# Tile 0's attention reordered on hand-assigned PSUM banks, and tile 1's query and key loaded once

## The chip, the cores and the metric

The kernel runs on one core of one Trainium2 chip. A core has five engines that work side by side and meet only at semaphores: TensorE (PE, matrix multiplies into PSUM), VectorE (DVE), ScalarE (ACT), GpSimd (POOL) and SyncE (SP). The metric is the device time of one execution in microseconds; lower is better. PSUM, where matmuls put their results, has eight banks of 128 partitions by 512 fp32 numbers in this kernel's use of it.

## What is computed

Sliding-window causal attention over 8 batches, 8 heads, 576 positions and head size 64 (window 64), followed by a gated feed-forward block on its 4608 x 512 result.

```python
scores = scale * np.matmul(q, k.transpose(0, 1, 3, 2))
rel = pos[:, None] - pos[None, :]
mask = (rel >= 0) & (rel < window)
scores = np.where(mask, scores, -1000000000.0)
attn = np.exp(scores - max); attn = attn / sum(attn)
x = np.matmul(attn, v)            # heads side by side: 4608 x 512
g = x @ w_gate
return (g / (1 + np.exp(-g)) * (x @ w_val)) @ w_out    # 512 -> 1536 -> 512
```

(`max` and `sum` stand for the row maximum and row sum.) Inputs and output are fp32; the kernel multiplies in bf16 and accumulates in fp32.

## The kernel before

The 4608 tokens are nine tiles of 512. Tiles 0 to 6 and 8 are the first 512 positions of a batch, tile 7 collects the last 64 positions of all eight. For each tile there is an attention stage (scores, exponential, totals, values) and a feed-forward stage: twelve gate groups m, each four matmuls for `g_ps` and four for `v_ps` (L412), then the projection `o_ps` (L421) with twelve steps c. Attention of tile t+1 is threaded between the projection matmuls of tile t.

The kernel runs under a manual schedule: every engine executes its instructions in the order in which the program text issues them. So a line's place in the text is its place in the engine's queue, and an instruction that waits holds up all behind it on that engine.

*Heads go in four pairs u = 0 to 3.* Tile 0 is special. Its q and k arrive as fp32 (`raw`), are cast to bf16 by ACT, DVE or POOL (`cast_first`), turned by PE against an identity matrix (`turn_pe`, L186) and copied out of PSUM into `qT` and `kT` (L546, L189). `scores_first` puts a bias matmul (L221, -1e9 outside the window) and 16 score matmuls (L230) into a two-bank tile and lets ACT exponentiate it. `log_of` and the lines before it form the totals with a matmul of ones (L287); ACT takes logarithm and then exp(-x), so that a multiplication replaces the division. `values_first` multiplies with the values (L337) and DVE scales the result into `xT` (L370). The value matmuls of tile 0 use blocks of 128 keys that begin either at a multiple of 128 (`v1`) or 64 rows before one (`v2`). `v2` is a copy of `v1` shifted by 64 partitions, made by `shift_pair` (L167, L168).

*Matmuls of ones* (`keep_warm`, L493) whose results nobody reads stand at some places of the opening.

*Tile 1.* Its key comes as `raw_k`, 128 partitions by heads, in bf16 by a converting DMA. During gate groups m = 5 to 9 of tile 0, ACT rearranges it (`join` into `keys`), PE turns it (L186, four transposes between two gate groups) and DVE copies it into `kT[1]`. Its query comes as `q_s` and is turned by DVE's 32 x 32 stream transpose (L198, `turn_q`) at m = 9, 10, 11 and after m = 11. That transpose needs the second 32 columns of each head on partitions 32 to 63 (and 96 to 127) at columns 0 to 31. So `load_q` sends the query twice: in four quarters, where the quarters c = 1 read the same rows from column 32 on. From tile 2 on the key is loaded in the same manner (`load_k`) and turned by DVE (L208, `turn_k`).

After the twelve groups of tile 0 comes the passage into tile 1, on PE in this order: `scores(1, 0)` (pairs 0 and 1), `columns(0, 4)` (16 projection matmuls), `scores(1, 1)` (pairs 2 and 3), `columns(4, 7)`, totals, `columns(7, 10)`, values, `columns(10, 12)`. For each `scores` call ACT exponentiates two tiles and DVE multiplies with the mask (L277) and adds (L282).

*PSUM* is given out by two pools: `ps_a` with two buffers of two banks (`wide`), `ps_f` with two tags "g" and "v" of two single banks each. A request takes the buffer of its tag that was asked for longest ago and waits until its readers are done.

*Loads.* POOL issues the weight and tile loads in the order of the text (L172, L74, L88, L178, L137); SP issues tile 0's q, k and half of v. Eight loads of POOL can be under way; the ninth waits for the first.

Of the kernel before, what the change touches and what calls it, by code (L numbers as in the profile page):

```python
# [8 lines left out]
P = 128  # L9
# [8 lines left out]
def kernel(  # L18
# [24 lines left out]
    hpool = ctx.enter_context(tc.tile_pool(name="hpool", bufs=2))  # L43
    ps_a = ctx.enter_context(tc.tile_pool(name="ps_a", bufs=2, space=PSUM))
    ps_f = ctx.enter_context(tc.tile_pool(name="ps_f", bufs=2, space=PSUM))

# [4 lines left out]
    v12 = cst.tile([P, 2, 4, H, D], BF16, name="v12")  # L51
    v1, v2 = v12[:, 0], v12[:, 1]
    vl = v12[:].rearrange("r g i (c w h) d -> r (g i) c w h d", c=2, w=2)
# [4 lines left out]
    tri = cst.tile([P, 2, 64], BF16, name="tri")  # L58
    bias = cst.tile([P, 2, 4, 4, 2, 16], BF16, name="bias")
    mask = cst.tile([P, 8, 2, 16, 4], BF16, name="mask")  # L60

# [19 lines left out]
    def load_q(t):  # L81

        q_s = stage.tile([P, 4, 16 * D], BF16, name="q_s", tag="q")
        w = 16 * D - 32
# [15 lines left out]
        return q_s  # L100

    def load_k(k_s, groups):

# [11 lines left out]
    def load_qk(t):  # L115
        q_s = load_q(t)
        if t == 1:
            staged[t] = q_s, None
            return
        if t == LAST:  # L120
# [42 lines left out]

    def shift_pair(u):
        hs = slice(2 * u, 2 * u + 2)
        a, b = v1[:, :, hs], v2[:, :, hs]
        nc.vector.tensor_copy(b[64:128, 1:4], a[64:128, 0:3])  # L167
        nc.vector.tensor_copy(b[0:64], a[0:64])  # L168

    def weights_gv(f0, f1, c0=0, c1=4):  # L170
# [41 lines left out]

    def scores_first(u):

        qT = queries[0][:, u, :]
        E = eb[u][:, 1:17].rearrange("r (h y) z -> r h (y z)", h=2)
        s_ps = wide("s_ps")
        for c in range(2):
            for h in range(2):
                r = slice(64 * h, 64 * h + 64)  # L220
                nc.tensor.matmul(  # L221
                    s_ps[64 * c:64 * c + 64, h], identb[r, r],
                    bias[r, c ^ h].rearrange("r e i c x -> r (e i c x)"),
                    start=True, stop=False,
                )
        for j in range(8):
            c = j % 2
            for h in range(2):
                r = slice(64 * h, 64 * h + 64)
                nc.tensor.matmul(  # L230
                    blocks(s_ps[64 * c:64 * c + 64, h], 0, j, min(8, j + 2)),
                    kT[0][r, u, 64 * j:64 * j + 64],
                    blocks(qT[r], 0, j, min(8, j + 2)),
                    start=False, stop=j > 5,
                )
        nc.scalar.activation(E, s_ps[:], AF.Exp, scale=0.125)
        weights[0, u] = E

# [5 lines left out]
    def scores(t, w):  # L244

        qT = queries[t]
        s_ps = [wide("s_ps") for _ in range(2)]
        for j in range(8):
# [76 lines left out]
    def sums_wide(t, w):  # L325
        d_ps, r = wide("d_ps"), room(2)
# [6 lines left out]
    def mix_first(u, o_ps):  # L333
        E = weights.pop((0, u))
        for m in range(8):
            for h in range(2):
                nc.tensor.matmul(  # L337
                    blocks(o_ps[half(h)], 0, m, m + 1),
                    (v2, v1)[m % 2][:, m // 2, 2 * u + h, :],
                    blocks(E[:, h, :], 0, m, m + 1),  # L340
                )

    def mix(t, w, o):
# [27 lines left out]

    def values_first(u, o_ps):
        mix_first(u, o_ps)
        scale(0, u, o_ps)

    def wide(name):
        return ps_a.tile([P, 2, 512], FP32, name=name, tag="a")

    def d_tile():
        return ps_f.tile([P, 512], FP32, name="d_ps", tag="v")[:]  # L380

    def mix_all(t):
        tiles = wide("ao_ps"), wide("ao_ps")
        for w in range(2):
# [12 lines left out]
    def gate_tiles():  # L397
        return [ps_f.tile([P, 512], FP32, name=x + "_ps", tag=x) for x in "gv"]

# [49 lines left out]
    def out_tile():  # L449
        return ps_f.tile([P, 512], FP32, name="o_ps", tag="g")  # L450

# [35 lines left out]
    make_identity(nc, identb[:])  # L487
    nc.vector.memset(v2[64:128, 0], 0.0)
    warm = ps_f.tile([P, 512], FP32, name="warm", tag="v")

# [32 lines left out]
    first = cast.tile([P, 2, 4, 4, 2 * D], BF16, name="qk_b", tag="c0")  # L523
    keys = cast.tile([P, 4, 4, 2 * D], BF16, name="k_b", tag="c1")
# [3 lines left out]
    def shift_dma(dst, src):  # L528
        nc.sync.dma_start(dst, src)

    def join(copy, dst, src):
        copy(dst.rearrange("r e (h d) -> r h e d", h=2), src)  # L532

    def one(name):
        return ps_a.tile([P, 2, 512], FP32, name=name, tag="a")[:, 0]

    casts = ((on_a, on_v), (on_p, on_a), (on_a, on_p), (on_v, on_a))

    def cast_first(u, i):
        join(casts[u][i], first[:, i, u], raw[i][:, 2 * u:2 * u + 2])  # L540

    def turn_pe(u):
        tps = [ps_f.tile([P, 512], BF16, name="tp", tag=x) for x in "gv"]
        for i in range(2):
            transposes(tps[i], first[:, i, u])
        (on_v if u else on_a)(queries[0][:, u, :], tps[0][:])  # L546
        split_k(kT[0][:, u, :], tps[1][:])

    cast_first(0, 0)
    cast_first(0, 1)  # L550
    turn_pe(0)
    cast_first(1, 0)
    cast_first(1, 1)
    load_v(nc.gpsimd, v1, (2, 3))
    keep_warm(1)
    scores_first(0)
    turn_pe(1)
    cast_first(2, 0)
    cast_first(2, 1)
    keep_warm(2)  # L560
    scores_first(1)
    cast_first(3, 0)
    cast_first(3, 1)
    turn_pe(2)
    keep_warm(1)
# [12 lines left out]
    weights_o(4, 8)  # L578
    weights_o(8, 12)
    load_halves(nc.gpsimd, vb[1], 1)  # L580
    for i in range(2):
        on_v(v1[:, i], v_first[:, i])
    scores_first(2)
    turn_pe(3)
    d_ps, r = wide("d_ps"), room(2)
    for u in range(2):
        totals_first(u, d_ps[:, u])
        inverse[0, u] = r[:, u]
    log(r, d_ps[:])
    invert(r)  # L590
    scores_first(3)

    def log_of(u):
        d_ps = one("d_ps")
        totals_first(u, d_ps)
        inverse[0, u] = room(1)[:, 0]
        log(inverse[0, u], d_ps)

    keep_warm(2)
    log_of(2)  # L600
    for u in range(2):
        shift_pair(u)
    for u in range(2):
        values_first(u, ps_f.tile([P, 512], FP32, name="ao_ps", tag="gv"[u])[:])
    for u in (2, 3):
        shift_pair(u)
    log_of(3)
    for u in (2, 3):
        invert(inverse[0, u])
    keep_warm(1)  # L610
    pairs = [gate_tiles() for _ in range(2)]
    for c in range(2):
        gate_part(0, (0, 1), pairs, c)
    for u in (2, 3):
        values_first(u, one("ao_ps"))
    for c in range(2, 4):
        gate_part(0, (0, 1), pairs, c)
    set_silu()
    for m in range(12):
# [4 lines left out]
        if m == 2:  # L624
# [20 lines left out]
    turn_q(1, 3)  # L645

    set_exp()
    tiles = [ps_f.tile([P, 512], FP32, name="o_ps", tag=x) for x in "gvgv"]

# [3 lines left out]
    scores(1, 0)  # L653
    columns(0, 4)
    scores(1, 1)
    columns(4, 7)
# [80 lines left out]
```

## Time and profile before

| what | value |
|---|---|
| median of 3 runs | 327.61 us (327.46 to 327.72) |
| profiled execution | 327.56 us |
| its span, first to last instruction | 325.6 us |
| PE busy in 0-10, 10-20, 20-30 us | 8.13, 8.22, 9.96 us |
| PE busy in 30-35, 35-40 us | 5.00, 4.63 of 5 us |
| DMA moved in 20-30 us | 201 GB/s |
| granted TensorE clock | 1.00 |

The span is what the profile covers; some two microseconds of the execution lie around it. A row of the order of time reads: start, time, engine, line, operation, output and input, count; in brackets the idle time of the engine just before and who ended it. Rows of matmuls overlap their neighbours, since the end of one is drawn while the next already runs: the step from start to start tells what one costs in a stream. Three more rows that the text refers to:

```
17.10 0.28 DVE L168 COPY v<-v 64x512 bf16<-64x512 bf16 x1
67.57 1.28 DVE L208 STREAM_TRANSPOSE kT<-k_s 128x512 bf16<-128x512 bf16 x1
29.26 0.39 PE L186 MATMUL tp<-identb,k_b 128*128 128x128 bf16 x4
```

### The profile page before, as it was taken

To read this page: it belongs to the slowest core of one execution; us is meant where nothing else is said; L and a number is where in the kernel's file an instruction comes from. 1 tells how busy PE (TensorE), PEld (TensorE's weight loads), DVE (VectorE), ACT (ScalarE), POOL (GpSimd) and SP (SyncE) were. 2 spreads that over 40 slices of the span, in tenths; PEclk is the share of its full clock that TensorE was granted. 3 is DMA by queue.
4 is the path that set the end of the run, shared out by engine and by line. 5 is a ranking of instruction groups with operands and counts; after the bars stand their busy time and mean duration, and the time that the engine had idled before them with its cause. 6 is when DMAs were issued, how large, how long until landed. Compare 5 with 4: busy or idle time off the path is not lost.

```text
span 325.6 us, 6987 instructions
## 1 busy us (share of the span) xinstructions
PE 318.5 (98%) x2743; PEld 150.6 (46%) x2743; DVE 219.7 (68%) x352; ACT 167.2 (51%) x239; POOL 143.0 (44%) x256
## 2 busy tenths in 40 slices
PE   7899999999999999999999999999999999999996
PEld 3444444444544454445444444444444544454443
DVE  4865755497767775887668766976787676774322
ACT  4954557337733683358436653566347633683310
POOL 4954445987086596575423999455200000000000
PEclk9999999999999999999999999999999999999999
DMA  7999999999779999969931999799501300021003
GB/s 250 202 202 201 206 144 192 188 134 151 166 148 208 128 175 171 196 70 215 204 62 18 154 186 94 50 179 198 121 3 29 96 8 2 8 83 42 2 18 112
DMA packets 82705, 40.84 MB, mean 125 GB/s; under 512 B 64112, under 2 KB 78192, under 8 KB 82672
## 3 DMA queue, kind: packets, MB, share of 16 engines
q0 software_dynamic: 50672, 23.08, 58.4%
q1 hardware_dynamic: 31456, 16.79, 20.5%
q10 hardware_dynamic: 544, 0.52, 0.5%
q8 instruction: 21, 0.34, 0.5%
q14 instruction: 12, 0.10, 0.1%
HBM read 54.00 MB, written 9.44 MB: 195 GB/s over the span
## 4 chain that ended last, share of the span: by engine, by line
PE 87%; DMA 8%; POOL 3%; DVE 1%; issue 0%; SPq 0%; DVEq 0%; POOLq 0%
PE o_ps L421 29%; PE g_ps L412 26%; PE v_ps L412 26%; DMA wv<-in_moe_w_val_dram 4%; DMA q_s<-in_q_dram 3%; PE s_ps L261 3%; PE ao_ps L354 2%; PE d_ps L294 1%; DMA q_f<-in_q_dram 1%; POOL wg L172 1%; POOL wv L172 1%; PE o_ps L463 1%; POOL v L129 1%; POOL qk_b L532 0%; DVE qT L198 0%
## 5 line engine op out<-in xcount | busy, mean ns | idle before, releaser
L405 ACT ACTIVATE sg<-g_ps 128x512 f32<-128x512 f32 x108 | 64.4, 597 | 113.8 <-PE g_ps L412 86.3
L406 DVE TENSOR_TENSOR hT<-sg,v_ps 128x512 bf16<-128x512 f32 x108 | 74.7, 693 | 59.3 <-PE v_ps L412 55.9
L412 PE MATMUL g_ps<-xT,wg 128*128 128x512 bf16 x424 | 108.8, 379 | 0.1
L412 PE MATMUL v_ps<-xT,wv 128*128 128x512 bf16 x424 | 108.8, 379 | 0.0
L421 PE MATMUL o_ps<-wo,hT 128*128 128x512 bf16 x420 | 95.2, 380 | 0.0
L108 POOL DMA_DIRECT2D k_s<-in_k_dram x112 | 60.6, 550 | 30.2 <-DMA q_s<-in_q_dram 18.1
L412 PEld LDWEIGHTS <-wv 128*128 128x128 bf16 x424 | 41.5, 98 | 50.2 <-issue 0.3
L412 PEld LDWEIGHTS <-wg 128*128 128x128 bf16 x424 | 41.3, 98 | 49.5 <-issue 0.6
L421 PEld LDWEIGHTS <-hT 128*128 128x128 bf16 x420 | 39.0, 98 | 46.6 <-issue 1.8
L274 ACT ACTIVATE eb<-s_ps 128x960 bf16<-128x960 f32 (+1 forms) x32 | 29.5, 975 | 16.5 <-PE s_ps L261 16.3
L208 DVE STREAM_TRANSPOSE kT<-k_s 128x512 bf16<-128x512 bf16 x28 | 36.0, 1285 | 1.0 <-DMA vb<-in_v_dram 1.0
L277 DVE TENSOR_TENSOR eb<-eb,mask 128x960 bf16<-128x960 bf16 (+1 forms) x32 | 21.1, 658 | 14.4 <-ACT eb L274 14.4
L370 DVE TENSOR_TENSOR xT<-ao_ps,r 128x512 bf16<-128x512 f32 x36 | 23.0, 685 | 6.6 <-PE ao_ps L354 4.8
L162 POOL CAST vb<-v_f 128x512 bf16<-128x512 f32 x20 | 11.5, 621 | 29.7 <-DMA v_f<-in_v_dram 17.9
L308 ACT ACTIVATE r<-d_ps 128x512 f32<-128x512 f32 (+1 forms) x33 | 20.8, 629 | 6.0 <-PE d_ps L294 5.9
L198 DVE STREAM_TRANSPOSE qT<-q_s 128x512 bf16<-128x512 bf16 x32 | 22.4, 702 | 0.9 <-DMA q_s<-in_q_dram 0.9
L311 ACT ACTIVATE r<-r 128x512 f32<-128x512 f32 (+1 forms) x33 | 22.0, 669 | 1.0
L88 POOL DMA_DIRECT2D q_s<-in_q_dram x28 | 15.2, 557 | 10.3 <-DVE qT L198 4.2
L137 POOL DMA_DIRECT2D vb<-in_v_dram x16 | 10.9, 692 | 9.3 <-DMA wo<-in_moe_w_out_dram 3.7
L282 DVE TENSOR_TENSOR both<-eb 128x512 bf16<-128x512 bf16 x32 | 13.6, 425 | 1.1
L471 ACT ACT_TABLE_LOAD x9 | 11.5, 1283 | 2.0 <-issue 1.9
L474 ACT ACT_TABLE_LOAD x9 | 11.5, 1283 | 0.2
(107 smaller groups left out, 182.4 us busy)
## 6 DMA issues: line engine op xcount, KB each, us to landing
q_s<-in_q_dram POOLq DMA_DIRECT2D x28, 248.0 KB, 6.3
k_s<-in_k_dram POOLq DMA_DIRECT2D x112, 56.0 KB, 4.8
v_f<-in_v_dram SPq DMA_DIRECT2D x40, 128.0 KB
wo<-in_moe_w_out_dram POOLq DMA_DIRECT2D x3, 512.0 KB, 12.3
q_f<-in_q_dram SPq DMA_DIRECT2D x4, 256.0 KB
vb<-in_v_dram POOLq DMA_DIRECT2D x16, 64.0 KB, 3.5
v<-in_v_dram POOLq DMA_DIRECT2D x16, 64.0 KB, 3.2
q_s<-in_q_dram POOLq DMA_DIRECT2D x16, 62.0 KB, 3.8
```

Source lines behind the costliest of these rows:

```text
L108: nc.gpsimd.dma_start(k_s[p0:p0 + 32, g, :, 0:w], k[b, a:H:2, s:s + P].rearrange("u (r e) d -> r u (e d)", e=4) [:, :, 32 * c:32 * c + w],)
L198: nc.vector.transpose(queries[t][:, u, :].rearrange("r (e x) -> r e x", e=16), staged[t][0][:, u].rearrange("r (e d) -> r e d", d=D)[:, :, ...
L208: nc.vector.transpose(dst[:, u, :].rearrange("r (g x e) -> r g e x", g=4, e=4), k_s[:, :, u].rearrange("r g (e d) -> r g e d", d=D)[:, :, ...
L274: nc.scalar.activation(flat, s_ps[h][:].rearrange("r a b -> r (a b)")[:, 0:n], AF.Exp, scale=0.125)
L277: nc.vector.tensor_mul(flat, flat, mask[:].rearrange("r j c e y -> r (j c e y)")[:, 0:n])
L308: nc.scalar.activation(r, d_ps, AF.Ln)
L311: nc.scalar.activation(r, r, AF.Exp, scale=-1.0)
L370: nc.vector.tensor_mul(x, o_ps, r)
L405: nc.scalar.activation(sg[:], g_ps[:], AF.Silu)
L406: nc.vector.tensor_mul(hT[t][:, m, :], sg[:], v_ps[:])
L412: nc.tensor.matmul(ps[:], w[:, c, P * m:P * m + P], xT[t][:, c, :], start=(c == 0), stop=(c == 3),)
L421: nc.tensor.matmul(o_ps[:], hT[t][:, c, P * s:P * s + P], wo[:, c, :], start=(c == 0), stop=(c == 11),)
```

## The change

*PSUM.* The two pools give way to eight fixed banks: `two[0]`, `two[1]` (two banks each, banks 0 to 3) and four single ones (4 to 7). Counters `taken` hand them out in turn for the rest of the kernel (`wide`, `out_tile`, `d_tile`).

*Opening.* Bias matmuls, score matmuls, exponential and totals are functions of their own, and are issued in another order; k of pair 2 and q and k of pair 3 are cast by DVE, q of pair 2 by POOL. `v2` and `shift_pair` are gone: a value matmul over a shifted block becomes two with half the rows each, which accumulate in PSUM (22 value matmuls for a pair, not 16). The parts of three pairs are issued together; a small marker matmul, read by DVE into `seen`, stands between the parts.

*Tile 1.* Key and query are loaded once, in plain layout. `second_halves` copies columns 32 to 63 of each head to the other 32 partitions: for the key by ACT (m = 7 to 10, two copies a pair), for the query by ACT and DVE (pairs 0 and 1, after m = 11) and by DVE alone (pairs 2 and 3, after `columns(0, 4)`). DVE turns the key (`turn_k`); PE's transposes, `raw_k` and `keys` are gone. The weight load 768:1280 is split in two, and the tile 1 loads stand between weight loads.

```diff
-    ps_a = ctx.enter_context(tc.tile_pool(name="ps_a", bufs=2, space=PSUM))
-    ps_f = ctx.enter_context(tc.tile_pool(name="ps_f", bufs=2, space=PSUM))
+    ps = ctx.enter_context(tc.tile_pool(name="ps", bufs=1, space=PSUM))
+    two = [ps.tile([P, 2, 512], FP32, name=f"two{i}") for i in range(2)]
+    bank = [two[i][:, j] for i in range(2) for j in range(2)]
+    bank += [ps.tile([P, 512], FP32, name=f"one{i}")[:] for i in range(4)]
...
+    def load_plain(t, which, us):
+        q_s, k_s = staged[t]
+        for a in range(2):
+            hs = slice(a + 2 * us.start, a + 2 * us.stop - 1, 2)
+            r = slice(64 * a, 64 * a + 32)
+            if which == "q":
+                nc.gpsimd.dma_start(
+                    q_s[r, us],
+                    q[batch(t), hs, 0:512].rearrange("u (r e) d -> r u (e d)", e=16),
+                )
+            else:
+                for u in range(us.start, us.stop):
+                    nc.gpsimd.dma_start(
+                        k_s[r, :, u],
+                        k[batch(t), 2 * u + a, 0:512].rearrange("(g r e) d -> r g (e d)", g=4, e=4),
+                    )
+
+    def second_halves(t, which, u, copies):
+        for a in range(2):
+            src, dst = slice(64 * a, 64 * a + 32), slice(64 * a + 32, 64 * a + 64)
+            if which == "q":
+                ap = staged[t][0][:, u].rearrange("r (e d) -> r e d", d=D)
+            else:
+                ap = staged[t][1][:, :, u].rearrange("r g (e d) -> r g e d", d=D)
+            half_d = (Ellipsis, slice(0, 32)), (Ellipsis, slice(32, 64))
+            copies[a](ap[dst][half_d[0]], ap[src][half_d[1]])
...
-    def shift_pair(u):
-        hs = slice(2 * u, 2 * u + 2)
-        a, b = v1[:, :, hs], v2[:, :, hs]
-        nc.vector.tensor_copy(b[64:128, 1:4], a[64:128, 0:3])
-        nc.vector.tensor_copy(b[0:64], a[0:64])
...
+    def mix_first(us, banks, mark):
+        def part(u, o_ps, x, m):
+            r = slice(0, P) if m % 2 else half(x)
+            E = weights[0, u]
             for h in range(2):
                 nc.tensor.matmul(
                     blocks(o_ps[half(h)], 0, m, m + 1),
-                    (v2, v1)[m % 2][:, m // 2, 2 * u + h, :],
-                    blocks(E[:, h, :], 0, m, m + 1),
-                )
+                    v1[r, m // 2 if m % 2 or not x else m // 2 - 1, 2 * u + h, :],
+                    blocks(E[r, h, :], 0, m, m + 1),
+                    start=m + x == 0, stop=(m, x) == (6, 1),
+                )
...
+        parts(0, (0, 2, 4, 6))
+        marker()
+        nc.vector.tensor_copy(seen[:], bank[mark][0:D, 0:1])
+        parts(0, (1, 3, 5, 7))
+        yield
+        marker()
+        parts(1, (2, 4, 6))
...
-    weights_gv(768, 1280)
-    raw_k = stage.tile([P, H, 4, D], BF16, name="k_r", tag="k")
-    for i in range(2):
-        hs = slice(4 * i, 4 * i + 4)
-        load_runs(nc.gpsimd, raw_k[:, hs], k, 1, hs)
+    weights_gv(768, 1024)
+    q_s = stage.tile([P, 4, 16 * D], BF16, name="q_s", tag="q")
+    k_s = stage.tile([P, 4, 4, 4 * D], BF16, name="k_s", tag="k")
+    staged[1] = q_s, k_s
+    load_plain(1, "k", slice(0, 2))
+    weights_gv(1024, 1280)
+    load_plain(1, "k", slice(2, 4))
     weights_gv(1280, 1536)
-    load_qk(1)
+    load_plain(1, "q", slice(0, 2))
     weights_o(0, 4)
+    load_plain(1, "q", slice(2, 4))
     weights_o(4, 8)
     weights_o(8, 12)
     load_halves(nc.gpsimd, vb[1], 1)
...
+    cast_first(on_v, 2, 1)
+    cast_first(on_v, 3, 0)
+    bias_first(1)
+    log0, inv0 = sums_first(0, 6)
+    scores_first(1)
+    log0()
+    weigh_first(1)
+    inv0()
+    keep_warm(1)
+    turn_first(2, (4, 5))
+    cast_first(on_v, 3, 1)
+    bias_first(2)
+    keep_warm(1)
+    log1, inv1 = sums_first(1, 7)
+    scores_first(2)
+    log1()
+    weigh_first(2)
+    inv1()
+    on_v(v1[:, 0], v_first[:, 0])
+    turn_first(3, (4, 5))
+    on_v(v1[:, 1], v_first[:, 1])
+    bias_first(3)
+    scores_first(3)
+    weigh_first(3)
+    log2, inv2 = sums_first(2, 6)
+    for _ in mix_first(range(3), (0, 1, 4), 7):
+        pass
+    log2()
+    inv2()
+    log3, inv3 = sums_first(3, 7)
+    log3()
+    inv3()
+    pairs = [(bank[2], bank[3]), (bank[0], bank[1])]
     for u in range(2):
+        scale(0, u, bank[u])
+    late = mix_first((3,), (5,), 6)
+    next(late)
     for c in range(2):
         gate_part(0, (0, 1), pairs, c)
+    for _ in late:
+        pass
     for u in (2, 3):
-        values_first(u, one("ao_ps"))
+        scale(0, u, bank[u + 2])
     for c in range(2, 4):
         gate_part(0, (0, 1), pairs, c)
...
-        if 5 <= m < 9:
-            u = m - 5
-            join(on_a, keys[:, u], raw_k[:, 2 * u:2 * u + 2])
-        if 6 <= m < 10:
-            u = m - 6
-            tp = ps_a.tile([P, 512], BF16, name="tp", tag="a")
-            transposes(tp, keys[:, u])
-            split_k(kT[1][:, u, :], tp[:])
-        if m >= 9:
-            turn_q(1, m - 9)
-    turn_q(1, 3)
+        if 7 <= m < 11:
+            second_halves(1, "k", m - 7, (on_a, on_a))
+            turn_k(kT[1], staged[1][1], m - 7)
+    for u in range(2):
+        second_halves(1, "q", u, (on_a, on_v))
+        turn_q(1, u)
...
     scores(1, 0)
     columns(0, 4)
+    for u in (2, 3):
+        second_halves(1, "q", u, (on_v, on_v))
+        turn_q(1, u)
     scores(1, 1)
     columns(4, 7)
```

More of the change, by code (lines that the diff above doesn't have):

```diff
@@ L51 @@
     v12 = cst.tile([P, 2, 4, H, D], BF16, name="v12")
-    v1, v2 = v12[:, 0], v12[:, 1]
+    v1 = v12[:, 0]
     vl = v12[:].rearrange("r g i (c w h) d -> r (g i) c w h d", c=2, w=2)
@@ L59 @@
     bias = cst.tile([P, 2, 4, 4, 2, 16], BF16, name="bias")
+    seen = cst.tile([D, 1], FP32, name="seen")
     mask = cst.tile([P, 8, 2, 16, 4], BF16, name="mask")
@@ L81, in load_q @@
     def load_q(t):
+        w = 16 * D - 32
         q_s = stage.tile([P, 4, 16 * D], BF16, name="q_s", tag="q")
-        w = 16 * D - 32
         for a, c in quarters:
@@ L116, in load_qk @@
         q_s = load_q(t)
-        if t == 1:
-            staged[t] = q_s, None
-            return
         if t == LAST:
@@ L211, in turn_k, with bias_first @@
         )
[L213 to L217, printed above, removed]
+    def bias_first(u):
         for c in range(2):
@@ L221, in scores_first @@
                 nc.tensor.matmul(
-                    s_ps[64 * c:64 * c + 64, h], identb[r, r],
+                    two[u % 2][64 * c:64 * c + 64, h], identb[r, r],
                     bias[r, c ^ h].rearrange("r e i c x -> r (e i c x)"),
@@ L225, in scores_first @@
                 )
+    def scores_first(u):
+        qT = queries[0][:, u, :]
         for j in range(8):
@@ L230, in scores_first @@
                 nc.tensor.matmul(
-                    blocks(s_ps[64 * c:64 * c + 64, h], 0, j, min(8, j + 2)),
+                    blocks(two[u % 2][64 * c:64 * c + 64, h], 0, j, min(8, j + 2)),
                     kT[0][r, u, 64 * j:64 * j + 64],
@@ L235, in scores_first @@
                 )
-        nc.scalar.activation(E, s_ps[:], AF.Exp, scale=0.125)
-        weights[0, u] = E
     quadrants = [(x, h) for h in range(2) for x in range(2)]
@@ L246, in scores @@
         qT = queries[t]
-        s_ps = [wide("s_ps") for _ in range(2)]
+        s_ps = wide(), wide()
         for j in range(8):
@@ L325, in sums_wide @@
     def sums_wide(t, w):
-        d_ps, r = wide("d_ps"), room(2)
+        d_ps, r = wide(), room(2)
         totals(t, w, (d_ps[:, 0], d_ps[:, 1]))
@@ L331, in sums_wide @@
         invert(r)
-    def mix_first(u, o_ps):
-        E = weights.pop((0, u))
-        for m in range(8):
+    def mix_first(us, banks, mark):
+        def part(u, o_ps, x, m):
+            r = slice(0, P) if m % 2 else half(x)
+            E = weights[0, u]
             for h in range(2):
@@ L338, in mix_first, with parts, marker @@
                     blocks(o_ps[half(h)], 0, m, m + 1),
-                    (v2, v1)[m % 2][:, m // 2, 2 * u + h, :],
-                    blocks(E[:, h, :], 0, m, m + 1),
-                )
+                    v1[r, m // 2 if m % 2 or not x else m // 2 - 1, 2 * u + h, :],
+                    blocks(E[r, h, :], 0, m, m + 1),
+                    start=m + x == 0, stop=(m, x) == (6, 1),
+                )
+        def parts(x, ms):
+            for u, b in zip(us, banks):
+                for m in ms:
+                    part(u, bank[b], x, m)
+        def marker():
+            nc.tensor.matmul(bank[mark][0:D, 0:16], ones[:, 0:D], ones[:, 0:16])
+        parts(0, (0, 2, 4, 6))
[5 more added lines that the diff above has]
+        parts(1, (2, 4, 6))
     def mix(t, w, o):
@@ L370, in scale, with take, wide @@
         nc.vector.tensor_mul(x, o_ps, r)
[L372 to L377, printed above, removed]
+    taken = {"a": 0, "g": 0, "v": 0}
+    def take(tag):
+        taken[tag] += 1
+        return taken[tag] % 2 ^ 1
+    def wide():
+        return two[take("a")]
     def d_tile():
-        return ps_f.tile([P, 512], FP32, name="d_ps", tag="v")[:]
+        return bank[6 + take("v")]
     def mix_all(t):
-        tiles = wide("ao_ps"), wide("ao_ps")
+        tiles = wide(), wide()
         for w in range(2):
@@ L397, in gate_tiles @@
     def gate_tiles():
-        return [ps_f.tile([P, 512], FP32, name=x + "_ps", tag=x) for x in "gv"]
+        return out_tile(), d_tile()
     def gate_end(t, m, pair):
@@ L449, in out_tile @@
     def out_tile():
-        return ps_f.tile([P, 512], FP32, name="o_ps", tag="g")
+        return bank[4 + take("g")]
     def project(t, s):
@@ L487 @@
     make_identity(nc, identb[:])
-    nc.vector.memset(v2[64:128, 0], 0.0)
-    warm = ps_f.tile([P, 512], FP32, name="warm", tag="v")
+    warm = bank[7]
     def keep_warm(n):
@@ L523 @@
     first = cast.tile([P, 2, 4, 4, 2 * D], BF16, name="qk_b", tag="c0")
-    keys = cast.tile([P, 4, 4, 2 * D], BF16, name="k_b", tag="c1")
     queries[0] = att.tile([P, 4, 512], BF16, name="qT", tag="qT")
     on_v, on_p, on_a = nc.vector.tensor_copy, nc.gpsimd.tensor_copy, nc.scalar.copy
[L528 to L543, printed above, removed]
+    def cast_first(copy, u, i):
+        copy(
+            first[:, i, u].rearrange("r e (h d) -> r h e d", h=2),
+            raw[i][:, 2 * u:2 * u + 2],
+        )
+    def turn_first(u, banks):
+        tps = [bank[b].bitcast(BF16)[:, 0:512] for b in banks]
@@ L544, in turn_pe, with weigh_first @@
         for i in range(2):
             transposes(tps[i], first[:, i, u])
[L546 to L554, printed above, removed]
+        (on_v if u else on_a)(queries[0][:, u, :], tps[0])
+        split_k(kT[0][:, u, :], tps[1])
+    def weigh_first(u):
+        E = eb[u][:, 1:17].rearrange("r (h y) z -> r h (y z)", h=2)
+        nc.scalar.activation(E, two[u % 2][:], AF.Exp, scale=0.125)
+        weights[0, u] = E
@@ L555, with sums_first @@
+    def sums_first(u, b):
+        totals_first(u, bank[b])
+        inverse[0, u] = room(1)[:, 0]
+        return lambda: log(inverse[0, u], bank[b]), lambda: invert(inverse[0, u])
+    cast_first(on_a, 0, 0)
+    cast_first(on_v, 0, 1)
+    turn_first(0, (4, 5))
+    cast_first(on_p, 1, 0)
+    cast_first(on_a, 1, 1)
+    load_v(nc.gpsimd, v1, (2,))
     keep_warm(1)
+    bias_first(0)
     scores_first(0)
[L557 to L565, printed above, removed]
+    weigh_first(0)
+    turn_first(1, (6, 7))
+    cast_first(on_p, 2, 0)
+    load_v(nc.gpsimd, v1, (3,))
     weights_gv(0, 256, 0, 2)
@@ L580 @@
     load_halves(nc.gpsimd, vb[1], 1)
-    for i in range(2):
-        on_v(v1[:, i], v_first[:, i])
-    scores_first(2)
-    turn_pe(3)
-    d_ps, r = wide("d_ps"), room(2)
-    for u in range(2):
[L587 to L611, printed above, removed]
+    cast_first(on_v, 2, 1)
[12 more added lines that the diff above has]
+    log1, inv1 = sums_first(1, 7)
+    scores_first(2)
+    log1()
[16 more added lines that the diff above has]
+    pairs = [(bank[2], bank[3]), (bank[0], bank[1])]
+    for u in range(2):
+        scale(0, u, bank[u])
+    late = mix_first((3,), (5,), 6)
+    next(late)
     for c in range(2):
         gate_part(0, (0, 1), pairs, c)
+    for _ in late:
+        pass
     for u in (2, 3):
-        values_first(u, one("ao_ps"))
+        scale(0, u, bank[u + 2])
     for c in range(2, 4):
@@ L634 @@
                 nc.vector.memset(E[:, 0], 0.0)
-        if 5 <= m < 9:
-            u = m - 5
-            join(on_a, keys[:, u], raw_k[:, 2 * u:2 * u + 2])
-        if 6 <= m < 10:
-            u = m - 6
-            tp = ps_a.tile([P, 512], BF16, name="tp", tag="a")
-            transposes(tp, keys[:, u])
-            split_k(kT[1][:, u, :], tp[:])
-        if m >= 9:
-            turn_q(1, m - 9)
-    turn_q(1, 3)
+        if 7 <= m < 11:
[4 more added lines that the diff above has]
+        turn_q(1, u)
     set_exp()
-    tiles = [ps_f.tile([P, 512], FP32, name="o_ps", tag=x) for x in "gvgv"]
+    tiles = [out_tile(), d_tile(), out_tile(), d_tile()]
     def columns(c0, c1):
```

## The prediction

> **What bounds the kernel now.** I read the busy line and the chain of waits first, then the order of time on PE, DVE and ACT from 0 to 60 us, and the landing records of the DMA queues.
>
> ```profile
> PE 318.5 (98%) x2743; PEld 150.6 (46%) x2743; DVE 219.7 (68%) x352; ACT 167.2 (51%) x239; POOL 143.0 (44%) x256
> PE 87%; DMA 8%; POOL 3%; DVE 1%; issue 0%; SPq 0%; DVEq 0%; POOLq 0%
> ```
>
> PE works 98% of the span and carries 87% of the chain; the rest of the chain lies before 40 us. From 40 us on the windows give PE 10.00 of 10 us almost throughout. So a delay of PE before 40 us moves the end one for one, and so does PE work removed there. Two places matter. The opening, where PE waits for the attention of tile 0:
>
> ```profile
> 13.17 0.41 PE L230 MATMUL s_ps<-qT,kT 64*64 64x128 bf16 x16 [0.79 <-DVE kT L189]
> 17.41 0.69 PE L337 MATMUL ao_ps<-eb,v 128*64 128x64 bf16 x32
> 18.71 0.38 PE L392 MATMUL g_ps<-xT,wg 128*128 128x512 bf16 x1 [0.60 <-DVE xT L370]
> 20.63 1.02 PE L412 MATMUL g_ps<-xT,wg 128*128 128x512 bf16 x4
> ```
>
> PE is idle 0.79 us for pair 3's keys and 0.60 us for xT; gate group m=2 starts at 20.63. Then the passage into tile 1, first PE, then DVE:
>
> ```profile
> 37.93 1.03 PE L412 MATMUL v_ps<-xT,wv 128*128 128x512 bf16 x4
> 39.49 0.61 PE L261 MATMUL s_ps<-qT,kT 64*64 64x128 bf16 x31 [0.36 <-DVE qT L198]
> 40.03 3.63 PE L421 MATMUL o_ps<-wo,hT 128*128 128x512 bf16 x16
> 43.59 0.62 PE L261 MATMUL s_ps<-qT,kT 64*64 64x128 bf16 x32
> ```
>
> ```profile
> 38.74 0.69 DVE L198 STREAM_TRANSPOSE qT<-q_s 128x512 bf16<-128x512 bf16 x1
> 39.36 0.65 DVE L406 TENSOR_TENSOR hT<-sg,v_ps 128x512 bf16<-128x512 f32 x1
> 39.93 1.29 DVE L198 STREAM_TRANSPOSE qT<-q_s 128x512 bf16<-128x512 bf16 x2
> 41.15 0.65 DVE L277 TENSOR_TENSOR eb<-eb,mask 128x960 bf16<-128x960 bf16 x1
> 42.85 0.42 DVE L282 TENSOR_TENSOR both<-eb 128x512 bf16<-128x512 bf16 x1
> ```
>
> The last gate matmul issues until E = 37.93 + 0.86 = 38.79 (0.864 is the step between groups of four). Tile 1's scores need two turned queries and wait 0.36 us for the second; columns(0,4) start at 40.03 = E + 1.24. The other two queries are turned at 39.93 to 41.2, while ACT does its exponentials, so scores(1,1) follow at 43.59 without a wait.
>
> **The change, part by part.**
>
> *Opening, -0.9 us.* Up to pair 0's exponential (ACT, 7.18) nothing moves. Then PE does the bias of pair 1, pair 0's totals (released at 8.20 by that exponential, 2 x 0.22) and pair 1's scores at 8.68. ACT's order becomes log0 8.92, exp1 9.47, inv0 10.39, log1 11.2, exp2 11.75, inv1, exp3 13.24, log2, inv2 (done 15.4), log3, inv3 (done 16.8), with the rows' slots of 0.92 for 1024 columns and 0.55 for 512. DVE gets one cast more (k2) and loses none that came before kT3: k2 8.53, q3 8.9, qT2 9.64, kT2 9.98, k3 10.67, v 11.02 (landed 10.53), qT3 11.7, kT3 12.04 to 12.72, v 12.7 to 13.1. Pair 3's scores start at 12.77, not 13.17. Pair 2's totals run to 13.54, then 66 value matmuls for three pairs. L337 prices one: 32 in 0.69 less 0.2 of drain is 0.016 us, 30 in 0.94 (with waits) less 0.2 is 0.025. At 0.02 PE is through at 14.9; xT0 14.95, xT1 15.6 to 16.25 (slots 0.6). Pair 3's totals and most of its values reach 15.7. Gate parts c=0 and c=1 are 8 x 0.216 us, the second pair from 16.3 since its two banks are one tile that xT1 still reads: done 17.6. The last six value matmuls end at 17.95 with drain, xT3 runs to 18.6, c=3 from 18.65 to 19.5, and m=2 starts there without waiting for a freed bank: 1.1 us early. At 0.025 us, and with each small step a little late, it is 20.0: 0.6 early. I take 0.9. Bounds: 0 (some step as late as today) and 2.7: wv for m=2 is recorded landed at 18.74, and its matmuls follow the gate's by 0.86, so m=2 gains nothing by starting before 17.9.
>
> *Shifted value copies out.* L167 and L168 are 8 instructions, 2.5 us of DVE, but DVE then idles 0.29 and 0.58 us for ao_ps: they end nothing, nor does the memset of the shifted block (0.27, ahead of a 0.48 wait). Six more value matmuls a pair (22 for 16) are in the sum above; the two `seen` reads fall in DVE gaps. The three warm matmuls fewer stood in PE's waits.
>
> *Loads.* Tile 1's query goes from 4 x 248 KB to 4 x 128 KB, key from 2 x 256 to 8 x 64 KB: 480 KB less, 2.3 us at the 206 GB/s of this stretch. POOL issues 12 DMAs for 6 at 0.55 to 0.79 us, and two more for the split weights; its queue is idle up to 3.04 us between issues there, so issue time is covered (uncovered: 8 x 0.55 = 4.4 us). By bytes in the queue, query pairs 0 and 1 land near 33.5, pairs 2 and 3 near 37.5; weights keep order and 1280:1536 lands near 32.5 for a need at 33.5. The landing at 37.41 that today holds DVE back goes; that gain is inside the next step.
>
> *Key transposes out, -0.92 us.* Four times PE does four 128x128 transposes between gate groups (29.26 to 29.49, 0.23 each), on the path. With the opening, E becomes 38.79 - 0.92 - 0.9 = 36.97.
>
> *First wait, +2.32 us.* For m = 7 to 10 ACT does two copies behind each sg (0.61 us rows of k_b, slots 0.5): done E(m) + 0.96. DVE turns a key block from E(m) + 1.0, slot 1.1 (L208: 67.57 to 68.66 before), so it is busy until E(m+1) + 0.37, and hT runs 0.1 late behind it. The two-bank rotation gives the next user of the v bank over 1.5 us, so PE doesn't feel it. But the query now comes wholly after m = 11: hT to E + 0.97, copy, turn, copy, turn. No row shows a copy of 32x512 bf16 from one partition group to another. Nearest is L168 (64x512, shifted partitions, 0.28). Bounds: 0.17 (L627, 64x64, four in 0.68) and 0.69 (L189, 512 strided columns out of PSUM). I take 0.28 since operands and length are L168's; a run of 32 in place of 128 columns is what the upper end is for. Copy ends E + 1.25, turn 1.30 to 1.99, copy 1.93 to 2.21, turn 2.26 to 2.95, scores from E + 3.0, columns from E + 3.56 against E + 1.24. Behind the waiting score matmul stands all of PE's work. ACT's two copies (by E + 0.96) and the table load (1.28) finish before the scores; uncovered, the load would cost its 1.28.
>
> *Second wait, +2.25 us.* Let S be the start of columns(0,4). Today DVE's last add of scores(1,0) issues at S + 2.82 and frees the engine at S + 3.16; scores(1,1) start at S + 3.56. Now four copies and two turns stand in that queue after the adds: copies 3.16 to 3.75, turn 3.80 to 4.49, copies 4.43 to 5.02, turn 5.07 to 5.76, scores S + 5.81. Work that lay under the exponentials lies behind them.
>
> Sum: -0.9 - 0.92 + 2.32 + 2.25 = +2.75 us. The profiled execution took 327.56 us, its span 325.6 and 1.96 around it; 330.31, and with the median 0.05 above that execution 330.4.
>
> A rule against the change: the trace starts cold, with L493's first six 512-column matmuls 0.43 us apart until 4.54 and 0.216 later, and its longest later gap, 0.79 us, changes nothing. The Trainium skill (TensorE: Matmul & The Clock Gate, "What's actually happening") says that TensorE falls back to half clock after an idle window of about 3.4 us. By that rule my gap of 2.9 us costs nothing, and one with slow copies about 1.7 us; no row here has such a gap.
>
> **Rivals.**
> - *Slow copies*: 0.69 us each. Six DVE copies lie on the path: 6 x 0.41 = +2.5, 332.9. For it: short runs, rows 32 partitions wide. Against: both operands bf16 in SBUF as in L168. 15%.
> - *PE cools* in the first wait. Price from the cold start: 3.4 us (1.13 to 4.54) at half rate, 1.7 us, so 332.1. For it: a gap nearly four times the longest of today. Against: 2.9 us is short of that 3.4, and 0.79 did nothing. 10%.
> - *The opening goes as far as weights let it*: m=2 at 17.9, 2.7 early: 328.6. Against: xT3's chain above. 3%.
> - *Not slower*: the same place decides. With both waits as priced, m=2 would have to start at 20.63 - (4.57 - 0.92) = 16.98 or earlier; at 16.5 the time is 327.1. For it: PE's waits there (0.22, 0.79 and 0.60 us) and seven warm matmuls of 0.22 us could go. Against: wv is recorded landed at 18.74, behind a queue that keeps its order. 10%, half of it beyond the margin.
> - *Forecast*: both waits, copies near 0.28: 62%, its own range 329.4 to 331.6 (opening 0 to 1.8, copies 0.17 to 0.35).
>
> **Numbers.** The likeliest gives 330.4. A range of 328.8 to 333.2 holds the forecast, the cooled clock and the slow copies, and leaves out what is not slower and slow copies together with cooling. A measurement here tells 0.2% (0.66 us) from no change. Faster 0.05, same 0.05, slower 0.90.
>
> **What would show it.** After: no L186 matmuls between gate groups; m=2's gate matmuls at 19.3 to 20.2; a PE wait of some 2.9 us ahead of tile 1's first scores and one of some 2.2 us ahead of the second, both put down to DVE qT; six DVE copies of q_s at 0.28 us; columns(0,4) near 40.5, the second scores near 46.3; from there the same picture 2.7 us later. Wrong if the second scores start at 43.6 or before, if the copies stand in another place on DVE, or if m=2 starts before 17.5.

## The result and the profile after

The changed kernel takes 331.8 us (median of 4 runs, 331.6 to 331.83) against 327.53 us (327.0 to 327.72) for the kernel before, measured beside it: ratio 1.0132, 95% interval 1.0114 to 1.0149. It is slower by 1.3%, as forecast; the time lies 1.4 us above the forecast of 330.4 us, just outside the forecast's own range (329.4 to 331.6) and inside the wide one (328.8 to 333.2). The profiled execution took 331.83 us with a span of 330.1, 4.27 us more than the one of before.

The busy line and the shares of the chain, after:

```profile
PE 316.4 (96%) x2709; PEld 150.7 (46%) x2751; DVE 223.5 (68%) x353; ACT 170.5 (52%) x245; POOL 147.8 (45%) x264
PE 84%; DMA 10%; POOL 3%; issue 1%; DVE 1%; SPq 0%; POOLq 0%
```

PE is busy 2.1 us less in a span 4.5 us longer: it waits more. The order of time on PE says where. First the opening, after (start, time, engine, line, operation, count, idle before):

```profile
12.52 0.41 PE L254 MATMUL two<-qT,kT 64*64 64x128 bf16 x16 [0.55 <-DVE kT L212]
17.64 0.28 PE L361 MATMUL one<-eb,v 64*64 64x64 bf16 x6
18.78 0.38 PE L435 MATMUL two<-xT,wg 128*128 128x512 bf16 x1
19.64 1.03 PE L455 MATMUL one<-xT,wg 128*128 128x512 bf16 x4
```

Pair 3's scores start at 12.52 for 13.17, the wait for xT3 is gone, and gate group m=2 starts at 19.64 for 20.63: 0.99 us gained. From there ten groups of 1.727 us follow with no transposes between them, and the last gate matmul has issued at E = 36.91 (before 38.79). Then the passage into tile 1 on PE, after:

```profile
39.96 0.21 PE L283 MATMUL two<-qT,kT 64*64 64x128 bf16 x1 [3.11 <-DVE qT L221]
41.24 0.79 PE L283 MATMUL two<-qT,kT 64*64 64x128 bf16 x31 [1.07 <-DVE qT L221]
41.96 5.08 PE L464 MATMUL one<-wo,hT 128*128 128x512 bf16 x16
46.97 0.24 PE L283 MATMUL two<-qT,kT 64*64 64x128 bf16 x1
47.97 0.62 PE L283 MATMUL two<-qT,kT 64*64 64x128 bf16 x31 [0.76 <-DVE qT L221]
57.74 1.02 PE L455 MATMUL one<-xT,wg 128*128 128x512 bf16 x4
```

The two waits that were forecast stand there, both ended by DVE's turned query. A third thing was a rival only: the sixteen matmuls of columns(0,4) take 5.0 us (41.96 to 46.97), not 3.56. From the second scores on everything is as before, 4.4 us later (tile 1's first gate group 57.74 for 53.37). Windows of two microseconds give the granted clock. Each line holds the stretch, its length, the busy time of PE, PEld, DVE, ACT and POOL with counts in brackets, and then the clock (0.88 in the first line; the last two numbers are of the DMA):

```profile
40.00:42.00 2.00, 0.93 (x33) 0.71 (x33) 1.08 (x2) 0.00 (x1) 0.41 (x2) 0.88 1.23 202
42.00:44.00 2.00, 2.00 (x7) 0.68 (x6) 0.93 (x2) 1.83 (x2) 0.53 (x1) 0.50 1.86 173
44.00:46.00 2.00, 2.00 (x8) 0.80 (x7) 1.87 (x6) 0.00 (x0) 1.36 (x3) 0.76 2.17 144
46.00:48.00 2.00, 1.24 (x10) 0.42 (x9) 1.84 (x4) 0.00 (x0) 1.55 (x3) 1.00 1.39 87
```

PE fell to half clock near 41.5 (a mean of 0.88 over two microseconds is 0.48 us at half) and came back near 45.0. Now what PE waited for, DVE and then ACT, after (`sg` is ACT's activation of a gate group, `hT` DVE's product of it with the values of the group):

```profile
35.05 1.33 DVE L231 STREAM_TRANSPOSE kT<-k_s 128x512 bf16<-128x512 bf16 x1
36.95 1.32 DVE L231 STREAM_TRANSPOSE kT<-k_s 128x512 bf16<-128x512 bf16 x1
38.08 0.71 DVE L449 TENSOR_TENSOR hT<-sg,one 128x512 bf16<-128x512 f32 x1
38.82 0.28 DVE L132 COPY q_s<-q_s 32x512 bf16<-32x512 bf16 x1
39.20 0.71 DVE L221 STREAM_TRANSPOSE qT<-q_s 128x512 bf16<-128x512 bf16 x1
39.94 0.43 DVE L132 COPY q_s<-q_s 32x512 bf16<-32x512 bf16 x1
40.48 0.71 DVE L221 STREAM_TRANSPOSE qT<-q_s 128x512 bf16<-128x512 bf16 x1
45.21 0.60 DVE L132 COPY q_s<-q_s 32x512 bf16<-32x512 bf16 x2
47.21 0.71 DVE L221 STREAM_TRANSPOSE qT<-q_s 128x512 bf16<-128x512 bf16 x1
```

```profile
33.14 0.60 ACT L448 ACTIVATE sg<-one 128x512 f32<-128x512 f32 x1
33.76 1.26 ACT L132 COPY k_s<-k_s 32x512 bf16<-32x512 bf16 x2
35.04 0.60 ACT L448 ACTIVATE sg<-one 128x512 f32<-128x512 f32 x1
```

ACT needs 1.90 us for a gate group (33.14 to 35.04) and is never idle in it, PE needs 1.73. DVE's turn starts at 35.05, when ACT's second copy has ended (35.02). So the key's turns fall behind, hT of m=11 starts at E + 1.17 and leaves DVE at E + 1.91, and only then comes the query.

### The profile page after: what moved, and what is told of

Its sections match the earlier page's. It is cut to its first block, busy times and chain, and to the rows that moved or that the text cites. A ratio compares the mean times of both kernels' runs of the same rounds, so it can differ in the third digit from the quotient of the medians.

```text
span 330.1 us, 6973 instructions
## 1 busy us (share of the span) xinstructions
PE 316.4 (96%) x2709; PEld 150.7 (46%) x2751; DVE 223.5 (68%) x353; ACT 170.5 (52%) x245; POOL 147.8 (45%) x264
## 4 chain that ended last, share of the span: by engine, by line
PE 84%; DMA 10%; POOL 3%; issue 1%; DVE 1%; SPq 0%; POOLq 0%
PE one L455 50%; PE one L464 27%; DMA wv<-in_moe_w_val_dram 4%; PE two L283 3%; DMA wo<-in_moe_w_out_dram 2%; PE two L395 2%; DMA vb<-in_v_dram 2%; DMA q_f<-in_q_dram 1%; PE one L316 1%; POOL wg L195 1%; PE one L506 1%; POOL wv L195 1%; POOL v L158 1%; DVE qT L221 0%; POOL qk_b L570 0%
## 5 line engine op out<-in xcount | busy, mean ns | idle before, releaser
L448 ACT ACTIVATE sg<-one 128x512 f32<-128x512 f32 x106 | 63.3, 597 | 109.5 <-PE one L455 82.2
L449 DVE TENSOR_TENSOR hT<-sg,one 128x512 bf16<-128x512 f32 x106 | 73.7, 695 | 57.1 <-PE one L455 56.2
L455 PE MATMUL one<-xT,wg 128*128 128x512 bf16 x416 | 108.4, 379 | 0.8
L455 PE MATMUL one<-xT,wv 128*128 128x512 bf16 x414 | 107.0, 379 | 0.1
L464 PE MATMUL one<-wo,hT 128*128 128x512 bf16 x397 | 95.1, 384 | 1.4 <-issue 0.3
L455 PEld LDWEIGHTS <-wg 128*128 128x128 bf16 x424 | 41.5, 98 | 50.2 <-issue 0.3
L455 PEld LDWEIGHTS <-wv 128*128 128x128 bf16 x424 | 41.5, 98 | 50.0
L296 ACT ACTIVATE eb<-two 128x960 bf16<-128x960 f32 (+1 forms) x32 | 29.5, 974 | 20.9 <-PE two L283 20.8
L411 DVE TENSOR_TENSOR xT<-two,r 128x512 bf16<-128x512 f32 x34 | 21.7, 686 | 6.4 <-PE two L395 4.8
L330 ACT ACTIVATE r<-one 128x512 f32<-128x512 f32 x32 | 18.9, 591 | 5.3 <-PE one L316 4.7
L283 PE MATMUL two<-qT,kT 64*64 64x128 bf16 (+1 forms) x576 | 10.7, 212 | 4.9 <-DVE qT L221 4.9
L283 PEld LDWEIGHTS <-kT 64*64 64x64 bf16 x576 | 8.4, 106 | 11.7 <-issue 11.3
```

What stands on the lines that cost most here:

```text
L283: nc.tensor.matmul(slot[:, o:o + 64 * n].rearrange("r (n e y) -> r e n y", n=n, e=16), src[half(h), 2 * w + x, k0:k0 + 64], blocks(qT[half ...
L296: nc.scalar.activation(flat, s_ps[h][:].rearrange("r a b -> r (a b)")[:, 0:n], AF.Exp, scale=0.125)
L411: nc.vector.tensor_mul(x, o_ps, r)
L448: nc.scalar.activation(sg[:], g_ps[:], AF.Silu)
L449: nc.vector.tensor_mul(hT[t][:, m, :], sg[:], v_ps[:])
L455: nc.tensor.matmul(ps[:], w[:, c, P * m:P * m + P], xT[t][:, c, :], start=(c == 0), stop=(c == 3),)
```

## The experiments

Times of one kernel spread more on the chips of the experiments (the kernel before: 327.05 to 328.27 on one of them). In the profile of *turns_first* the opening's matmuls ran slow up to 10 us and m=2 started at 21.32, not 19.64. So beside the time I use the *passage*: from the last gate matmul of tile 0 to tile 1's first gate matmul on PE. It is 53.37 - 38.79 = 14.58 us before and 57.74 - 36.91 = 20.83 us after; the opening and the twelve gate groups are not in it.

| run | time us (range) | ratio to before | passage us |
|---|---|---|---|
| changed kernel | 331.8 (331.6 to 331.83) | 1.0132 | 20.83 |
| warm | 332.19 (331.56 to 332.79) | 1.0141 | 21.86 |
| turns_first | 331.5 (330.6 to 333.24) | 1.0127 | 20.55 |
| turns_first_warm | 329.48 (328.93 to 330.49) | 1.0058 | 18.09 |
| keys_early | 331.25 (331.0 to 332.62) | 1.0122 | 20.55 |
| open_only | 327.74 (327.2 to 328.36) | 1.0008 | 14.63 |
| tile1_only | 332.96 (332.47 to 333.15) | 1.0165 | 20.91 |
| early_all | 325.91 (325.73 to 326.12) | 0.9955 | 14.79 |
| early_split | 325.57 (324.92 to 325.66) | 0.9939 | 14.50 |

### What does the half clock cost?

```diff
+    for _ in range(14):
+        nc.tensor.matmul(two[0][0:D, 0], ones[:, 0:D], ones[:])
     scores(1, 0)
```

> The changed kernel with 14 warm matmuls of 512 columns (3.0 us) on PE between the last gate group of tile 0 and tile 1's first scores, where PE waits 4.3 us anyway. Theory A (the end is set by DVE's queue of copies and turns; the half clock of the columns after the first wait lies inside the second wait): the 32 scores go from 0.72 to 0.55 us and columns(0,4) from 5.0 to 3.6 us, the wait ahead of the second scores grows from 1.0 to 2.4 us, and the time falls by the scores' 0.17 only, 331.6. Theory B (the cooled clock is what the prediction lacked): the time falls by the whole 1.6 us, 330.2.

PE after the warm matmuls, and three windows of the same profile:

```profile
41.55 3.63 PE L464 MATMUL one<-wo,hT 128*128 128x512 bf16 x15
47.59 0.61 PE L283 MATMUL two<-qT,kT 64*64 64x128 bf16 x31 [1.12 <-DVE qT L221]
49.83 2.75 PE L464 MATMUL one<-wo,hT 128*128 128x512 bf16 x6 [0.22 <-issue]
```

```profile
46.00:48.00 2.00, 0.65 (x30) 0.52 (x32) 1.45 (x4) 0.00 (x0) 1.45 (x3) 1.00 1.39 101
48.00:50.00 2.00, 1.78 (x24) 0.90 (x14) 0.73 (x2) 1.77 (x2) 1.39 (x3) 0.76 1.06 157
50.00:52.00 2.00, 2.00 (x6) 0.61 (x4) 1.35 (x3) 0.06 (x1) 1.53 (x4) 0.50 1.10 203
```

Columns(0,4) are back at full speed (41.55, second scores could follow at 45.1), and the second scores come at 47.59 all the same: DVE isn't ready. Theory B is out. But theory A's small gain doesn't show either: the second wait has grown past 2 us, PE's clock falls after it instead (near 49.0), and the half clock now lies on columns(4,7), where nothing hides it. The lower two of the four times (331.56, 331.74; mean granted clock 0.999 and 0.998) are theory A's 331.6; the other two, the profiled execution of 332.79 among them, have the cooling (0.995).

The other edit, alone and with the warm matmuls:

```diff
+    for u in (2, 3):
+        second_halves(1, "q", u, (on_v, on_v))
+        turn_q(1, u)
     scores(1, 0)
     columns(0, 4)
-    for u in (2, 3):
-        second_halves(1, "q", u, (on_v, on_v))
-        turn_q(1, u)
     scores(1, 1)
```

> The changed kernel with the copies and turns of query pairs 2 and 3 issued ahead of the first scores call, so that on DVE they stand before its masks and adds and lie under the exponentials. Theory A: the second wait goes, but the slow columns(0,4) are then uncovered: second scores at 47.0 for 47.97, time 1.0 us less, 330.8. Rival (clock plays no part, columns slow only because PE has nothing urgent): 2.4 us less, 329.4. Rival (place in the queue is not the cause): no change, 331.8.

> Both edits: the pairs 2 and 3 turned ahead of the masks, and 14 warm matmuls in the first wait. Theory A: what each hides from the other is gained together: columns from 41.8 at full clock, second scores at 45.3, time 2.6 us less than the changed kernel, 329.2; more than the sum of the two edits alone (0.2 + 1.0). If the two are independent: their sum, 330.6.

PE in turns_first, then in turns_first_warm:

```profile
43.72 5.69 PE L464 MATMUL one<-wo,hT 128*128 128x512 bf16 x16
49.34 0.62 PE L283 MATMUL two<-qT,kT 64*64 64x128 bf16 x32
```

```profile
41.49 3.63 PE L464 MATMUL one<-wo,hT 128*128 128x512 bf16 x15
45.04 0.62 PE L283 MATMUL two<-qT,kT 64*64 64x128 bf16 x32
```

In both the second wait is gone, the scores follow the columns without idle time. Alone, the edit shows the slow columns in full (5.6 us from start to start), and the passage is only 0.28 us shorter, where 1.0 us was expected: the half clock lasted 6.8 us here, from 41.1 to 47.9, and not 3.4. Its times spread over 2.6 us and settle nothing by themselves. With the warm matmuls the passage is 2.74 us shorter than the changed kernel's, and the time of 329.48 us (interval 1.0036 to 1.0081) agrees with theory A's 329.2 and not with the 330.6 of two independent gains. The two cover each other: DVE's late queue hid the slow columns, and the slow columns hid how late the queue was.

### Is the first wait ACT's doing?

```diff
-        if 7 <= m < 11:
+        if 5 <= m < 9:
```

with the pair numbers shifted to fit.

> The changed kernel with the key's copies and turns at gate groups m = 5 to 8 in place of 7 to 10. Theory A (ACT's two copies at 0.62 us a slot make its round 1.90 us against PE's 1.73, so hT of m = 11 came 0.9 us late and the query behind it): hT(11) starts 0.3 us after the last gate matmul for 1.17, first scores about 0.9 us sooner, time 330.8 to 330.9. Rival (only the query's own copies and turns after m = 11 count): no change, 331.8.

DVE from the last gate group on, and three windows, in keys_early:

```profile
37.10 0.69 DVE L449 TENSOR_TENSOR hT<-sg,one 128x512 bf16<-128x512 f32 x1 [1.04 <-PE one L455]
37.82 0.50 DVE L132 COPY q_s<-q_s 32x512 bf16<-32x512 bf16 x1
39.16 0.55 DVE L132 COPY q_s<-q_s 32x512 bf16<-32x512 bf16 x1
46.85 0.71 DVE L221 STREAM_TRANSPOSE qT<-q_s 128x512 bf16<-128x512 bf16 x1
```

```profile
38.00:40.00 2.00, 0.21 (x1) 0.10 (x1) 1.77 (x4) 1.23 (x1) 1.59 (x3) 0.84 1.24 209
40.00:42.00 2.00, 1.43 (x33) 1.03 (x33) 0.52 (x1) 0.41 (x1) 0.38 (x1) 0.50 1.24 207
46.00:48.00 2.00, 1.99 (x35) 0.89 (x36) 1.48 (x4) 0.00 (x0) 1.23 (x3) 0.96 1.38 127
```

The last gate matmul has issued at 36.83 and hT starts 0.27 us later, idle before it: without the late key there is no lag. So the key's copies and turns at m = 7 to 10 made it. The run moves ACT's copies and DVE's turns together; that ACT's round and not DVE's is the slow one is read from the order of time of the changed kernel, where ACT is never idle and DVE's turn starts as ACT's copy ends. Of the 0.9 us the first scores gain 0.6 against E (3.74 for 4.33 us), because the copies took 0.50 and 0.55 us here, not 0.28 and 0.43. PE stays at half clock until 46.2: the first scores take 0.95 us for 0.72, and DVE's queue behind them ends with the last turn at 47.56, so the passage falls by 0.28 us only. The time, 331.25 us (interval 1.0088 to 1.0156), doesn't tell theory and rival apart; the profile does.

### The two halves of the change apart

*open_only* has the new opening and the old tile 1. Against the changed kernel:

```diff
-    load_plain(1, "k", slice(0, 2))
...
-    load_plain(1, "k", slice(2, 4))
...
+    for i in range(2):
+        hs = slice(4 * i, 4 * i + 4)
+        load_runs(nc.gpsimd, raw_k[:, hs], k, 1, hs)
     weights_gv(1280, 1536)
-    load_plain(1, "q", slice(0, 2))
+    load_qk(1)
     weights_o(0, 4)
-    load_plain(1, "q", slice(2, 4))
...
-            second_halves(1, "k", m - 7, (on_a, on_a))
-            turn_k(kT[1], staged[1][1], m - 7)
...
+            transposes(tp, keys[:, u])
+            split_k(kT[1][:, u, :], tp)
```

*tile1_only* is the kernel before, with its opening and its pools, and the same lines of tile 1 exchanged the other way round:

```diff
-    load_qk(1)
+    load_plain(1, "q", slice(0, 2))
     weights_o(0, 4)
+    load_plain(1, "q", slice(2, 4))
...
-            transposes(tp, keys[:, u])
-            split_k(kT[1][:, u, :], tp[:])
...
+            second_halves(1, "k", m - 7, (on_a, on_a))
+            turn_k(kT[1], staged[1][1], m - 7)
```

> The changed opening alone: banks, order, no shifted copies; tile 1 loaded, turned on PE and copied as in the kernel before. Theory A (the query's last quarter lands at 37.4 us whatever PE does, since the loads keep their bytes and order): gate groups 1.0 us earlier, the whole gain goes into the wait for the turned query ahead of tile 1's scores (0.36 to about 1.4 us), columns(0,4) at 40.0 as before, time within 0.2 us of the kernel before. Rival (the opening's gain stands by itself): 1.0 us faster than before.

> Tile 1's single loads, copies and turns alone, with the opening of the kernel before. Theory A: the whole loss and without the opening's 1.0 us, since here the loads are early enough for PE to be late: 1.0 us slower than the changed kernel, 332.8. Rival (part of the loss comes from the opening or from the hand-given banks): at or below 331.8.

PE and one line of ACT in open_only:

```profile
29.02 0.40 PE L212 MATMUL two<-identb,k_b 128*128 128x128 bf16 x4 [0.53 <-ACT k_b L689]
39.29 0.61 PE L286 MATMUL two<-qT,kT 64*64 64x128 bf16 x31 [0.40 <-DVE qT L224]
```

```profile
28.35 0.62 ACT L689 COPY k_b<-k_r 128x512 bf16<-128x512 bf16 x1 [1.81 <-DMA k_r<-in_k_dram]
```

The time is that of before (1.0008, interval 0.9998 to 1.0019), as theory A has it, but the gain goes at another place than it said. m=2 starts at 19.70, 0.93 us early. Then ACT waits 1.81 us for the key's landing at 28.35 and PE behind it; the last gate matmul is only 0.24 us early, and the wait for the query, which lands about when it did before, stays at 0.40. Once the opening is faster, the loads set the pace up to 40 us.

tile1_only is 332.96 us where 332.8 was expected (1.0165, interval 1.015 to 1.018), and its passage is that of the changed kernel. So the loss belongs to tile 1 alone, and the opening gives 1 us only where the loads are fewer too.

### A version that beats both

*early_all* moves the key to m = 5 to 8 and the copies of pairs 2 and 3 ahead of the scores, as above, and the query of pairs 0 and 1 into the loop:

```diff
+        if m == 9:
+            for u in range(2):
+                second_halves(1, "q", u, (on_a, on_v))
+            for u in range(2):
+                turn_q(1, u)
```

*early_split* also cuts the first load of w_out:

```diff
-    weights_o(0, 4)
+    weights_o(0, 2)
     load_plain(1, "q", slice(2, 4))
+    weights_o(2, 4)
```

> The changed kernel with all of tile 1's copies and turns moved ahead of where they are waited for: key at m = 5 to 8, query pairs 0 and 1 at m = 9, pairs 2 and 3 ahead of the first scores call. Theory A (place in ACT's and DVE's queues is all that was wrong): first scores within 0.3 us of the last gate matmul, no cooled clock, pairs 2 and 3 turned at 41.8 since their query lands at 39.0, second scores at 41.9 against 43.6 before: 1.7 us faster than before, 325.9. Rival (the copies on chip cost more than the loads save, wherever they stand): not faster than before.

> early_all with the first load of w_out cut in two and the query of pairs 2 and 3 loaded between the halves. Theory A (what is left of the second wait in early_all is the landing of that query at 39.0): it lands near 37.5, second scores at 41.2, 0.7 us less than early_all, 325.2. Rival (DVE's queue, not the landing, holds the second scores in early_all): no difference.

PE and DVE in early_split, and last a row of DVE in early_all:

```profile
36.98 0.86 PE L283 MATMUL two<-qT,kT 64*64 64x128 bf16 x32
37.77 3.63 PE L464 MATMUL one<-wo,hT 128*128 128x512 bf16 x16
41.33 0.67 PE L283 MATMUL two<-qT,kT 64*64 64x128 bf16 x32
```

```profile
40.62 0.71 DVE L221 STREAM_TRANSPOSE qT<-q_s 128x512 bf16<-128x512 bf16 x1
```

```profile
39.00 0.43 DVE L132 COPY q_s<-q_s 32x512 bf16<-32x512 bf16 x1 [0.28 <-DMA q_s<-in_q_dram]
```

The first scores follow the last gate matmul (36.89) at once, the second ones follow the columns, and the last query is turned at 41.33, just then. early_all takes 325.91 us (ratio 0.9955, interval 0.9943 to 0.9968), early_split 325.57 (0.9939, interval 0.9926 to 0.9953): 0.6% faster than before with the same copies on chip. The load order was worth less than the 0.7 us expected: the passage is 0.29 us shorter than early_all's. In early_all DVE waited only 0.28 us for the query's landing; the rest is its queue of four copies and two turns. early_all's second scores already started at 41.27 and took 0.87 us up to the next matmul, for 0.60 in early_split.

## Why the prediction was right, and where it was short

| step | predicted us | measured us | from |
|---|---|---|---|
| opening | -0.9 | -0.99 | m=2 at 19.64 for 20.63 |
| key transposes | -0.92 | -0.89 | E 36.91 for 38.79, less the opening |
| first wait | +2.32 | +3.81 | E to columns: 5.05 for 1.24 |
| second wait | +2.25 | +2.45 | columns to second scores: 6.01 for 3.56 |
| sum | +2.75 | +4.38 | second scores 47.97 for 43.59 |

The mechanism held: PE work before 40 us moves the end one for one, and two waits for the turned query cost more than the opening and the transposes give. The opening was right to 0.1 us: its steps had been followed engine by engine with the rows' slots, and the last of them, c=3, starts at 18.78 for 18.65. That 0.9 was taken, between the 0.6 and 1.1 worked out, was a choice.

The term that was mis-sized is the first wait, by 1.5 us, in three parts. The largest, 0.94: "slots 0.5" for ACT's copies, taken from full-width rows that overlap their neighbours by 0.1 us. These copies to other partitions didn't overlap; each kept ACT for 0.62 us, a round of sg and two copies 1.90 us. So hT came 0.28 us later than predicted in the first of the four rounds and 0.17 more in each of the next three, 0.8 in all, where I had a steady lag of 0.1; the rest is hT itself, which kept DVE for 0.74 us and not 0.6. keys_early, with the key out of the way, has no such lag. Then 0.39 in the copies and turns after hT, which followed each other without overlap as well, one copy at 0.43. Then 0.16 from the scores, whose last part ran at half clock. The second wait is 0.2 us longer than predicted, since its copies and turns didn't overlap either.

The rival "PE cools" came true, with the forecast instead of in its place. Its price was about right (columns 1.45 us longer and scores 0.17, for 1.7), yet the second wait, predicted for a warm PE, absorbed the 1.45: it starts when the first scores end and runs on DVE whatever the columns do. warm shows it. To list it as a separate case, whose price comes on top of the forecast, was the mistake. So was the reason against it, that a gap of 2.9 us is too short to cool PE: in warm a pause of 2.5 us was enough. The slow copies at 0.69 didn't occur; the DVE copies took 0.28 to 0.55. The loads were hidden here, and open_only shows what they cover; the query of pairs 2 and 3 landed at 39.0 and not near 37.5, which cost nothing, since DVE got to it at 45.21.

That the time stayed within the range was in part luck. The range was wide for the cooled clock and for slow copies on DVE; the larger part of what was missing came from ACT's copies, for which no rival had a price.

## What to carry to other kernels

When a copy is moved from a DMA onto engines, ask first where it stands in the in-order queue of each engine; the same copies lengthened the passage by 6.25 us in one place and not at all in another (early_split: 14.50 us for 14.58). A gain ahead of a stage whose pace is set by loads is kept only if the loads get earlier too. And two delays that lie over each other must be removed together: taken out one at a time, each looked worthless here.

## What was not expected of the hardware

PE's clock fell after shorter pauses than I had allowed for, and it fell by half. By the windows it was down from about 41.5 to 45.0 in the changed kernel, 4.6 us after the last gate matmul with one score matmul and the first of the other 31 between, and from about 39.4 to 46.2 in keys_early, 2.5 us after it with one score matmul between. In turns_first no matmul lies between: the last gate matmul has issued at 38.59, the next matmul starts at 41.64, and the clock is down from about 41.1, again after 2.5 us:

```profile
40.00:42.00 2.00, 0.26 (x1) 0.12 (x1) 1.75 (x4) 1.67 (x2) 0.48 (x1) 0.78 1.24 209
```

In warm it fell near 49.0, 1.4 us after the matmuls had set in again behind a pause of 2.5 us with one matmul in it. The time at half clock was 3.4 us in the changed kernel and in warm, and 6.8 us in turns_first, keys_early and tile1_only. The Trainium skill (TensorE: Matmul & The Clock Gate, "What's actually happening") gives a free-running window of about 3.4 us, idle for the fall and busy for the return. The lengths at half clock agree with one and two such windows; the fall 2.5 us into a pause doesn't agree with a whole idle window.

A copy of 32x512 bf16 to the next partition group took 0.28 to 0.55 us on DVE. What makes it slow was not tried.
